# One attention-and-gating block on one core: the row maximum over two key blocks formed as relu of a score difference, kept in its PSUM bank, with the second scores accumulated onto it

## The chip, the cores and the metric

The kernel runs on one core of one Trainium2 chip. The metric is device microseconds (us) of one launch. The kernel before takes 1705.86 us (median of three runs, 1705.18 to 1706.04). Engine names here are those of the profile: PE is TensorE (PEld its weight loads), ACT is ScalarE, DVE is VectorE, POOL is GpSimd, SP issues most DMAs.

## The reference, cut to what matters

The block has 2048 rows of width 512, 32 heads of 16, and a gated MLP behind the attention.

```python
h  = x + softmax((ln(x) @ wq) @ (ln(x) @ wk).T * 16**-0.5) @ (ln(x) @ wv) @ wo   # 32 heads
z  = gelu(ln(h) @ w_in);  z1, z2 = z[:, :688], ln(z[:, 688:])
out = h + (z1 * (w_sp @ z2 + b_sp)) @ w_out
```

A softmax needs the maximum of each row of 2048 scores before its exponentials. This change concerns how that maximum is found.

## The kernel before, in words

**Stages.** The kernel first normalizes x and projects queries, keys and values (until about 158 us). Then it runs the attention proper (about 158 to 1300 us), then h and z row block by row block (about 1300 to 1455 us), then the spatial product and the output.

**Attention.** A unit is a group of four heads (`hg`), 512 queries (`qb`) and 128 keys (`kb`). The loop at L1086 takes two units at a time, 256 such rounds, in the order that the list `PAIR` (L40) writes out by hand:

```python
PAIR = "s0 M0 join s2 M4 M1 s1 H s3 invert M2 s5 M3 H out M5 s4 M7 turn s6 s7 M6 P".split()
```

- `s0` to `s7` (L846) are the eight score matmuls of the two units. Each fills one of three PSUM banks `s`, and ACT exponentiates it into `pt` in SBUF (L855).
- `H` (twice) weighs the values of the second unit of the round before with half of the columns each, `P` those of this round's first unit (L871): four float32 matmuls, eight rows in the trace, on bank `pv`.
- `M0` to `M7` are the steps of `max_pair` (L205). They find the row maxima of 128 queries of two heads, one of each kind named below, and run eleven rounds ahead of the scores that need them.
- `out` copies `pv` away on DVE (L881, once in eight rounds), `invert`, `join` and `turn` do small work on DVE, each once in eight rounds.

**The row maxima.** The four heads of a unit are of two kinds, `t` = 0 and 1, which lie on different halves of PE's rows (0 to 49 and 64 to 113). So a matmul of one kind can run beside one of the other. A step makes the scores of 128 queries for 512 keys in a bank `m0` to `m3` (L223), and DVE takes the maximum of each row (`reduce_max`, L228). For `t` = 1 that is done for all four blocks of keys (M0, M4, M5, M7), for `t` = 0 for the last two (M1, M2). The first two blocks of `t` = 0 go by max(a, b) = (a + b + |a - b|) / 2. Keys are added and subtracted beforehand (`uvs`, made in `sums`, L480, and loaded by `load_uv`, L170). M3 (`minus`, L230) makes a - b, and ACT writes |a - b| to an SBUF tile `ab` (L233). M6 (`plus`, L235) makes a + b in another bank, and DVE adds `ab`, halves and takes the maximum in one custom instruction (L237), followed by one that reads its accumulator.

**Banks and queues.** Each step takes the next of the four `m` banks in turn (L1145). In a round, M0, M4, M1, M2, M3, M5, M7, M6 take banks 0, 1, 2, 3, 0, 1, 2, 3. Instructions stand on every engine in the order in which the program gives them; a matmul that waits holds up the matmuls behind it.

**Before and after the loop.** The first eleven rounds' worth of maxima are found during the projections (`ahead`, L544), in calls of five or four steps. The last eleven rounds have no `M` steps. In the z stage the pool `mid_ps` (L1220) has six banks, shared by the four accumulators of z in a row block and the one of h (L1310).

In what follows a prime marks the round that comes next: s0' is its first score matmul.

Of the kernel before, what the change touches and what calls it, by code (L numbers as in the profile page):

```python
# [19 lines left out]
P = 128  # L20
# [39 lines left out]
def block_kernel(ctx: ExitStack, tc: tile.TileContext, x, wqkv, wo, w_in, w_sp4, b_sp, w_out, out):  # L60
# [20 lines left out]

    q_scr = dram.tile([2, H * DH, S], F16, name="q_scr")
    k_scr = dram.tile([2, H * DH, S], F16, name="k_scr")
    uv_scr = dram.tile([2, DB, P // 2, 2, 512], F16, name="uv_scr")
    v_scr = dram.tile([S, D], F32, name="v_scr")
    o_scr = dram.tile([DB, 8, 32, S], F32, name="o_scr")
    r_scr = dram.tile([H, S], F32, name="r_scr")
# [54 lines left out]
    VP = NB * 4 * VW  # L142
    vst = [vpool.tile([P, VP + DH], F32, name=f"vst{i}") for i in range(2)]
    kst = [kpool.tile([RG + KM, 2, S], F16, name="kst0")]
    uvs = [kpool.tile([KS, 2, 1024], F16, name="uvs0")]
    qst, mx, turned = {}, {}, {}

    def fixed(t):
# [21 lines left out]
    def load_uv(hg, pieces=range(3)):  # L170
        r = slice(32 * (hg % 2), 32 * (hg % 2) + 32)
        for j in pieces:
            nc.sync.dma_start(
                uvs[hg % 2][j:KS:3, :, :],
                uv_scr[(0, 0, 1)[j], hg // 2, r].rearrange("(p r) i s -> r p (i s)", r=DH))

    def load_v(hg):
        raw = vpool.tile([P, NB, 4 * DH], F32, name="raw")
# [26 lines left out]
    def max_pair(m):  # L205

        g, i = divmod(m, 8)
        hg, qb = divmod(g, NQ)
        q, k, w = qst[g], kst[hg % 2], uvs[hg % 2]
        if i == 0:
            mx[g] = sm.tile([P, 16, 4], F32, name="mx")
            nc.gpsimd.memset(mx[g][:, :8, 3:], LOW)
        c, p = slice(i % 4 * P, i % 4 * P + P), i // 4
        at = lambda t, e: mx[g][:, t * 8 + i, e:e + 1]

        def scores(t, keys, b):  # L220
            r = slice(RG * t, RG * t + KS)
            acc = bank(b)
            nc.tensor.matmul(acc, q[r, p, c], keys[r, p], start=True, stop=True)  # L223
            return acc

        def one(t, e, b):
            acc = scores(t, k[:, :, 512 * e:512 * e + 512], b)
            nc.vector.reduce_max(at(t, e if t else e - 1), acc, axis=AX.X)  # L228

        def minus(b):  # L230
            acc = scores(0, w[:, :, 512:], b)
            ab[0] = sm.tile([P, 512], F32, name="ab")
            nc.scalar.activation(ab[0], acc, AF.Abs)  # L233

        def plus(b):  # L235
            acc = scores(0, w[:, :, :512], b)
            nc.vector.tensor_tensor_reduce(ab[0], acc, ab[0], 0.5, LOW, ALU.add, ALU.max, at(0, 0))  # L237

        def finish():
            if i == 7:  # L240
                nm = sm.tile([P, 2, 8], F32, name="nm")
                nc.vector.tensor_reduce(nm.rearrange("p t i -> p (t i)"), mx.pop(g), axis=AX.X,  # L242
                                        op=ALU.max, negate=True)
                parts = sm.tile([P, 2, 2, 8], F16, name="mparts")
                nc.gpsimd.tensor_scalar(nm, nm, 1.0 / ONE, 1.0, op0=ALU.mult, op1=ALU.mult)  # L245
                nc.gpsimd.tensor_copy(parts[:, :, 0], nm)
                nc.gpsimd.tensor_sub(parts[:, :, 1], nm, parts[:, :, 0])
                turned[0] = (g, parts)

        ab = {}  # L250
        four = [lambda b, e=e: one(1, e, b) for e in range(4)]
        two = [lambda b, e=e: one(0, e, b) for e in (2, 3)]
        return [four[0], two[0], two[1], minus, four[1], four[2], plus, four[3], finish]

    def max_rows():

# [12 lines left out]
    with ExitStack() as pre:  # L269
# [188 lines left out]
        def proj_qk(b, n, which, between=lambda d: None):  # L458

            c = slice(n * 512, (n + 1) * 512)  # L460
            acc = next_acc()
            for d in range(DB):
                mm3(acc, wqk[b][0][:, which, d, :], wqk[b][1][:, which, d, :],
                    xT[0][:, d, c], xT[1][:, d, c], d == 0, d == DB - 1)
                between(d)

            def take(by_act=True):
                part = p2.tile([P, 2, 512], F16, name="part", bufs=PB)
                if by_act:
                    nc.scalar.activation(part[:, 0, :], acc, AF.Copy, scale=QK_DOWN)  # L470
                else:
                    nc.vector.tensor_scalar(part[:, 0, :], acc, QK_DOWN, None, op0=ALU.mult)
                nc.vector.scalar_tensor_tensor(part[:, 1, :], acc, QK_DOWN, part[:, 0, :],
                                               op0=ALU.mult, op1=ALU.subtract)
                scr = (q_scr, k_scr)[which]
                nc.sync.dma_start(scr[:, b * P:(b + 1) * P, c].rearrange("i p s -> p i s"), part)
                if which == 1 and n < 2:
                    rest.append(sums)

            def sums():  # L480
                hh = P // 2
                if which == 1 and n < 2:
                    kf[n] = p2.tile([P, 512], F32, name=f"kf{n}", bufs=1)
                    nc.scalar.activation(kf[n][:hh], acc[:hh], AF.Copy, scale=QK_DOWN)
                    nc.scalar.activation(kf[n][hh:], acc[:hh], AF.Copy, scale=-QK_DOWN if n else QK_DOWN)
                if which == 1 and n == 1:
                    uv = p2.tile([P, 512], F32, name="uv", tag="row", bufs=10)
                    nc.gpsimd.tensor_add(uv, kf[0], kf[1])
                    part = p2.tile([P, 2, 512], F16, name="part", bufs=PB)
                    nc.gpsimd.tensor_copy(part[:, 0, :], uv)  # L490
                    nc.gpsimd.tensor_sub(part[:, 1, :], uv, part[:, 0, :])
                    for i in range(2):
                        nc.sync.dma_start(uv_scr[:, b, :, i, :].rearrange("i p s -> p i s"),
                                          part[hh * i:hh * i + hh])

            return take

# [46 lines left out]
        def ahead(k):  # L544
            for _ in range(k):
                m = done[0] // 8
                if not todo and m < LEAD:
                    steps = max_pair(m)
                    todo.extend(steps[i] for i in (0, 1, 4, 2, 5, 3, 6, 7))
                    ends.append(steps[8])  # L550
                if todo:
                    todo.pop(0)(done[0] % 5)
                    done[0] += 1
                    if not todo:
                        ends.pop()()
# [273 lines left out]
    with ExitStack() as at:  # L829
        kpool1 = at.enter_context(tc.tile_pool(name="kpool1", bufs=1))  # L830
        kst.append(kpool1.tile([RG + KM, 2, S], F16, name="kst1"))
        uvs.append(kpool1.tile([KS, 2, 1024], F16, name="uvs1"))
        fixed(kst[1])
        pp = at.enter_context(tc.tile_pool(name="pp", bufs=6))
        ps_v = at.enter_context(tc.tile_pool(name="ps_v", bufs=1, space=PSUM))
# [381 lines left out]
    with ExitStack() as mid:  # L1217
        m2 = mid.enter_context(tc.tile_pool(name="mid_2", bufs=2))
        zs, zst = {}, {}
        ps = mid.enter_context(tc.tile_pool(name="mid_ps", bufs=6, space=PSUM))  # L1220

        def new_z(sb):
            zs[sb] = [m2.tile([P, FH], F32, name=f"z{i}", bufs=1 + 3 * i) for i in range(2)]
# [75 lines left out]
        with tc.manual_schedule(engines={E.PE, E.Activation, E.DVE, E.Pool, E.SP}):  # L1299
            asked.pop(0)()  # L1300
            load_row(row[4])
            for k in range(NB):
                sb, new = row[k], row.get(k + 2)
                if k >= NB - 2:
                    scale_z(row[k - 1])
                    gate_z(row[k - 1])
                if k + 4 < NB:
                    asked.pop(0)()
                if k and new is not None:
                    for _ in make_h(new, ps.tile([P, 512], F32, name="acc")):  # L1310
                        pass
                if k + 3 < NB:
                    split_o(row[k + 3])
                if k + 5 < NB:
                    asked.append(load_o(row[k + 5]))
                new_z(sb)
                for c in range(2):
                    make_z(sb, 1, c)
                if new is not None:
                    mv, rs = scale_h(new)  # L1320
                    nb = minus_mean(e2, mv, rs)
                mean_z(sb)
                if 0 < k < NB - 2:
                    scale_z(row[k - 1])
                if new is not None:
                    hns[new] = e2.tile([P, D], F32, name="hn")
                    nc.scalar.activation(hns[new], xrs.pop(new), AF.Identity, bias=nb, scale=rs)
                    halve_h(new)
                spread_z(sb)
                if new is not None:  # L1330
                    turn_h(new)
                if subs:
                    subs.pop()(nc.vector)
                if k + 5 < NB:
                    load_row(row[k + 5])
                if k % 2:
                    ask()
                for c in range(2):
                    make_z(sb, 0, c)
                nc.scalar.dma_start(z_scr[sb * P:(sb + 1) * P, :], zs[sb][0])  # L1340
                hTs.pop(sb)
                if k == 1:
                    invert()
                if 0 < k < NB - 2:
                    gate_z(row[k - 1])
# [319 lines left out]
```

## Time and profile before

| | |
|---|---|
| median of three runs | 1705.86 us |
| the profiled execution | 1703.25 us |
| its span (first to last instruction) | 1701.5 us |
| mean granted PE clock | 1.00 |
| exponentials on ACT (L855), attention | 1968, mean 638 ns |
| row maxima on DVE (L228) | 1510, mean 682 ns |
| the custom instruction on DVE (L237) | 252 with `m` banks, mean 676 ns |
| absolute values on ACT (L233) | 252 with `m` banks, mean 626 ns |

A row of the timeline gives a start, a length, the engine, the line, the operation, output and inputs with shapes, and how many instructions were merged. A length is from start to end of an instruction: on all three engines the next one starts before the last has ended, so the distance of two starts is shorter than a length. Here the distance of two starts, or of two ends, in a full queue is called a slot.

### The profile page before, as it was taken

To read this page: it belongs to the slowest core of one execution; us is meant where nothing else is said; L and a number is where in the kernel's file an instruction comes from. 1 tells how busy PE (TensorE), PEld (TensorE's weight loads), DVE (VectorE), ACT (ScalarE), POOL (GpSimd) and SP (SyncE) were. 2 spreads that over 40 slices of the span, in tenths; PEclk is the share of its full clock that TensorE was granted. 3 is DMA by queue.
4 is the path that set the end of the run, shared out by engine and by line. 5 is a ranking of instruction groups with operands and counts; after the bars stand their busy time and mean duration, and the time that the engine had idled before them with its cause. 6 is when DMAs were issued, how large, how long until landed. Compare 5 with 4: busy or idle time off the path is not lost.

```text
span 1701.5 us, 36391 instructions
## 1 busy us (share of the span) xinstructions
PE 1687.1 (99%) x13410; PEld 634.3 (37%) x13410; DVE 1431.4 (84%) x3011; ACT 1338.1 (79%) x2648; POOL 821.8 (48%) x1070
## 2 busy tenths in 40 slices
PE   9999999999999999999999999999999999999999
PEld 4433222222222222222222222222224666666665
DVE  7588999999999999999999999999955776543444
ACT  4335999999999999999999999999996677211111
POOL 1522867776673266687767777400001778200100
PEclk9999999999999999999999999999999999999999
DMA  5744332343221244344443544300116775664551
GB/s 186 205 113 143 99 89 80 91 94 85 79 66 26 57 119 118 92 147 133 123 124 105 147 143 127 87 14 13 40 34 150 203 198 144 235 229 157 202 215 44
DMA packets 214138, 202.29 MB, mean 119 GB/s; under 512 B 92328, under 2 KB 164840, under 8 KB 213960
## 3 DMA queue, kind: packets, MB, share of 16 engines
q1 hardware_dynamic: 211656, 194.33, 39.9%
q10 hardware_dynamic: 2304, 5.64, 1.1%
q8 instruction: 105, 1.72, 0.4%
q14 instruction: 73, 0.60, 0.1%
HBM read 122.10 MB, written 65.93 MB: 111 GB/s over the span
## 4 chain that ended last, share of the span: by engine, by line
PE 85%; DVE 8%; POOL 2%; DMA 2%; ACT 1%; issue 1%; SPq 1%; POOLq 0%; ACTq 0%
PE pv L871 26%; PE s L846 18%; PE m L223 10%; DVE mx L228 6%; PE acc L107 5%; PE acc L109 5%; PE acc L108 5%; PE g L107 4%; PE g L108 4%; PE g L109 4%; PE acc L772 2%; DVE og L881 1%; DVE ab L237 1%; ACT pt L855 1%; DMA raw<-in_w_sp 0%
## 5 line engine op out<-in xcount | busy, mean ns | idle before, releaser
L855 ACT ACTIVATE pt<-s 128x512 f32<-128x512 f32 x1968 | 1007.1, 638 | 2.7 <-PE m L223 1.5
L228 DVE TENSOR_REDUCE mx<-m 128x1 f32<-128x512 f32 x1510 | 947.0, 682 | 11.8 <-PE m L223 3.0
L846 PE MATMUL s<-qst,kst 50*128 50x512 f16 x2048 | 604.2, 379 | 0.1
L871 PE MATMUL pv<-pt,vst 128*32 128x256 f32 (+1 forms) x6056 | 598.2, 466 | 4.1 <-DVE og L881 1.2
L223 PE MATMUL m<-kst,qst 48*128 48x512 f16 x1510 | 452.4, 381 | 0.1
L846 PEld LDWEIGHTS <-kst 50*128 50x128 f16 x2048 | 131.8, 94 | 352.0 <-issue 323.6
L871 PEld LDWEIGHTS pv<-pt,vst 128*32 128x32 f32 x6056 | 119.5, 108 | 290.0 <-issue 276.6
L223 PEld LDWEIGHTS <-qst 48*128 48x128 f16 x2048 | 159.4, 93 | 174.5 <-issue 124.0
L223 PE MATMUL m<-uvs,qst 48*128 48x512 f16 x504 | 190.7, 380 | 0.4 <-DVE mx L228 0.4
L245 POOL TENSOR_SCALAR nm<-nm 128x16 f32<-128x16 f32 x32 | 6.5, 204 | 361.2 <-DVE nm L242 361.2
L237 DVE CUSTOM_DVE_ANT_0 ab<-m,ab 128x512 f32<-128x512 f32 x252 | 170.3, 676 | 2.7 <-ACT ab L233 2.7
L233 ACT ACTIVATE ab<-m 128x512 f32<-128x512 f32 x252 | 157.8, 626 | 15.8 <-PE m L223 15.1
L1429 ACT ACTIVATE pr<-pr,up 128x304 f32<-128x304 f32 (+1 forms) x32 | 17.0, 574 | 108.7 <-DVE up L1383 108.7
L1032 POOL TENSOR_TENSOR op<-raw,op 128x512 f16<-128x512 f32 x80 | 92.8, 1160 | 6.1
L955 POOL TENSOR_TENSOR raw<-raw 128x512 f32<-128x512 f32 (+1 forms) x84 | 83.1, 989 | 6.7
L960 POOL TENSOR_TENSOR acc_sp<-acc_sp,raw 128x512 f32<-128x512 f32 x63 | 80.3, 1275 | 4.5
L107 PE MATMUL acc<-wi,hT 128*128 128x344 f16 x256 | 79.1, 309 | 3.0 <-DVE xr L776 3.0
L109 PE MATMUL acc<-wi,hT 128*128 128x344 f16 x256 | 79.1, 309 | 0.0
L108 PE MATMUL acc<-wi,hT 128*128 128x344 f16 x256 | 79.1, 309 | 0.0
L1571 POOL TENSOR_TENSOR pr<-pr,z 128x344 f32<-128x344 f32 x8 | 7.3, 910 | 148.4 <-DMA whole<-squares 108.3
L952 POOL TENSOR_SCALAR raw<-raw 128x512 f32<-128x512 f32 (+1 forms) x88 | 52.1, 592 | 19.8 <-DMA raw<-in_wqkv 12.5
L1570 DVE TENSOR_TENSOR pr<-g,v 128x344 f32<-128x344 f32 x8 | 4.1, 516 | 66.3 <-PE g L109 63.5
(253 smaller groups left out, 2280.5 us busy)
## 6 DMA issues: line engine op xcount, KB each, us to landing
raw<-in_w_sp SPq DMA_DIRECT2D x128, 256.0 KB
s_scr<-op SPq DMA_DIRECT2D x64, 256.0 KB
op<-s_scr SPq DMA_DIRECT2D x32, 512.0 KB
a_scr<-op SPq DMA_DIRECT2D x48, 256.0 KB
op<-a_scr SPq DMA_DIRECT2D x24, 512.0 KB
o_scr<-og SPq DMA_DIRECT2D x64, 128.0 KB
qst<-q_scr SPq DMA_DIRECT2D x192, 32.0 KB
kst<-k_scr SPq DMA_DIRECT2D x48, 128.0 KB
```

The costliest lines, as they stand in the source:

```text
L107: nc.tensor.matmul(ps, lh, rh, start=first, stop=False, **kw)
L108: nc.tensor.matmul(ps, lh, rl, start=False, stop=False, **kw)
L109: nc.tensor.matmul(ps, ll, rh, start=False, stop=last, **kw)
L223: nc.tensor.matmul(acc, q[r, p, c], keys[r, p], start=True, stop=True)
L228: nc.vector.reduce_max(at(t, e if t else e - 1), acc, axis=AX.X)
L233: nc.scalar.activation(ab[0], acc, AF.Abs)
L237: nc.vector.tensor_tensor_reduce(ab[0], acc, ab[0], 0.5, LOW, ALU.add, ALU.max, at(0, 0))
L846: nc.tensor.matmul(s, kst[hg % 2][r, p, kb * P:(kb + 1) * P], qst[hg * NQ + qb][r, p, :], start=True, stop=True)
L855: nc.scalar.activation(pts[p, kb][:, t, :], s, AF.Exp, scale=scales_[hg // 2])
L871: nc.tensor.matmul(pv[0][32 * j:32 * j + 32, a:b], vst[hg % 2][:, c:c + 32], pts[j % 2, kb][:, j // 2, a:b], start=kb == 0, stop=kb == NB - 1,
L955: pool.tensor_mul(got[0] if n else acc, got[0], got[0])
L1032: chores.append((lambda: pool.tensor_sub(t[0][:, 1], of(), t[0][:, 0]), TT))
```

## The change

The difference a - b stays in its bank: ACT writes relu(a - b) over it in place (step 3, now `over`). Step 6, now `onto`, multiplies the queries with the second block of the keys themselves and accumulates onto the same bank: relu(a - b) + b = max(a, b). DVE takes the maximum with the same `reduce_max` as elsewhere. The sum of keys is no longer made, stored or loaded, and the tile `ab` is gone. `onto` takes no bank of its own, though the count that hands out banks still advances. `PAIR` is not changed. In the calls during the projections, step 3 now comes fourth and step 2 fifth. In the z stage, h has a bank of its own and z's accumulators five.

```diff
-        def minus(b):
-            acc = scores(0, w[:, :, 512:], b)
-            ab[0] = sm.tile([P, 512], F32, name="ab")
-            nc.scalar.activation(ab[0], acc, AF.Abs)
-
-        def plus(b):
-            acc = scores(0, w[:, :, :512], b)
-            nc.vector.tensor_tensor_reduce(ab[0], acc, ab[0], 0.5, LOW, ALU.add, ALU.max, at(0, 0))
+        def over(b):
+            both[0] = scores(0, w, b)
+            nc.scalar.activation(both[0], both[0], AF.Relu)
+
+        def onto(b):
+            r = slice(0, KS)
+            nc.tensor.matmul(both[0], q[r, p, c], k[r, p, 512:1024], start=False, stop=True,
+                             skip_group_check=True)
+            nc.vector.reduce_max(at(0, 0), both[0], axis=AX.X)
...
-        return [four[0], two[0], two[1], minus, four[1], four[2], plus, four[3], finish]
+        return [four[0], two[0], two[1], over, four[1], four[2], onto, four[3], finish]
...
                 if which == 1 and n < 2:
-                    kf[n] = p2.tile([P, 512], F32, name=f"kf{n}", bufs=1)
-                    nc.scalar.activation(kf[n][:hh], acc[:hh], AF.Copy, scale=QK_DOWN)
-                    nc.scalar.activation(kf[n][hh:], acc[:hh], AF.Copy, scale=-QK_DOWN if n else QK_DOWN)
+                    kf[n] = p2.tile([hh, 512], F32, name=f"kf{n}", bufs=1)
+                    nc.scalar.activation(kf[n], acc[:hh], AF.Copy, scale=QK_DOWN)
...
-                    todo.extend(steps[i] for i in (0, 1, 4, 2, 5, 3, 6, 7))
+                    todo.extend(steps[i] for i in (0, 1, 4, 3, 2, 5, 6, 7))
...
-        ps = mid.enter_context(tc.tile_pool(name="mid_ps", bufs=6, space=PSUM))
+        ps = mid.enter_context(tc.tile_pool(name="mid_ps", bufs=5, space=PSUM))
+        ps_h = mid.enter_context(tc.tile_pool(name="mid_h", bufs=1, space=PSUM))
...
-                    for _ in make_h(new, ps.tile([P, 512], F32, name="acc")):
+                    for _ in make_h(new, ps_h.tile([P, 512], F32, name="h")):
```

PE, from the last score matmul of a round (s7) over M6 and P to the first two matmuls of the next round (s0' and M0'), in the kernel before; a number behind a name tells one buffer from another:

```order
L846 LDWEIGHTS kst1_1822
L846 MATMUL s_9679<-qst_7925,kst1_1822 128x512 [waits Activation_49]
L223 LDWEIGHTS qst_8499
L223 MATMUL m3_9682<-uvs1_1823,qst_8499 128x512 [waits DVE_49]
L871 MATMUL pv_9685<-pt_9620,vst1_157 32x512 [waits DVE_49]
L871 MATMUL pv_9685<-pt_9627,vst1_157 32x512
L871 MATMUL pv_9685<-pt_9620,vst1_157 32x512
L871 MATMUL pv_9685<-pt_9627,vst1_157 32x512
L846 LDWEIGHTS kst1_1822
L846 MATMUL s_9722<-qst_7925,kst1_1822 128x512 [waits Activation_49]
L223 LDWEIGHTS qst_8499
L223 MATMUL m0_9725<-kst1_1822,qst_8499 128x512
```

The same place in the changed kernel:

```order
L844 LDWEIGHTS kst1_1788
L844 MATMUL s_9436<-qst_7729,kst1_1788 128x512 [waits Activation_49]
L236 LDWEIGHTS qst_8287
L236 MATMUL m0_9412<-kst1_1788,qst_8287 128x512 [waits Activation_49]
L869 MATMUL pv_9441<-pt_9378,vst1_157 32x512 [waits DVE_49]
L869 MATMUL pv_9441<-pt_9385,vst1_157 32x512
L869 MATMUL pv_9441<-pt_9378,vst1_157 32x512
L869 MATMUL pv_9441<-pt_9385,vst1_157 32x512
L844 LDWEIGHTS kst1_1788
L844 MATMUL s_9478<-qst_7729,kst1_1788 128x512 [waits Activation_49]
L223 LDWEIGHTS qst_8287
L223 MATMUL m0_9481<-kst1_1788,qst_8287 128x512 [waits DVE_49]
```

The rows stand in the same order. M6 writes bank 0, which M3 filled, and waits for ACT in place of DVE; M0', which takes bank 0 in its turn, now waits for DVE.

DVE, from M2's maximum over those of M5, M7 and M6 to M0', in the kernel before, in a round with the copy of `pv`:

```order
L228 TENSOR_REDUCE mx_9375<-m3_9647 128x1 [waits PE_49]
L881 COPY og_9662<-pv_9066 128x512 [waits PE_49]
L228 TENSOR_REDUCE mx_9375<-m1_9666 128x1 [waits PE_49]
L228 TENSOR_REDUCE mx_9375<-m2_9672 128x1 [waits PE_49]
L237 ISA ab_9656,mx_9375<-m3_9682,ab_9656 128x512 [waits PE_49,Activation_49]
L237 ISA mx_9375 128x1
L228 TENSOR_REDUCE mx_9375<-m0_9725 128x1 [waits PE_49]
```

The same place in the changed kernel:

```order
L228 TENSOR_REDUCE mx_9139<-m3_9405 128x1 [waits PE_49]
L879 COPY og_9419<-pv_8838 128x512 [waits PE_49]
L228 TENSOR_REDUCE mx_9139<-m1_9423 128x1 [waits PE_49]
L228 TENSOR_REDUCE mx_9139<-m2_9429 128x1 [waits PE_49]
L238 TENSOR_REDUCE mx_9139<-m0_9412 128x1 [waits PE_49]
L228 TENSOR_REDUCE mx_9139<-m0_9481 128x1 [waits PE_49]
```

One plain reduction stands in place of the custom instruction and its reader. The last maximum of a round and the first of the next read the same bank.

More of the change, by code (lines that the diff above doesn't have):

```diff
@@ L83, in block_kernel @@
     k_scr = dram.tile([2, H * DH, S], F16, name="k_scr")
-    uv_scr = dram.tile([2, DB, P // 2, 2, 512], F16, name="uv_scr")
+    uv_scr = dram.tile([2, DB, P // 2, 512], F16, name="uv_scr")
     v_scr = dram.tile([S, D], F32, name="v_scr")
@@ L144, in block_kernel @@
     kst = [kpool.tile([RG + KM, 2, S], F16, name="kst0")]
-    uvs = [kpool.tile([KS, 2, 1024], F16, name="uvs0")]
+    uvs = [kpool.tile([KS, 2, 512], F16, name="uvs0")]
     qst, mx, turned = {}, {}, {}
@@ L174, in load_uv @@
                 uvs[hg % 2][j:KS:3, :, :],
-                uv_scr[(0, 0, 1)[j], hg // 2, r].rearrange("(p r) i s -> r p (i s)", r=DH))
+                uv_scr[(0, 0, 1)[j], hg // 2, r].rearrange("(p r) s -> r p s", r=DH))
     def load_v(hg):
@@ L248, in finish @@
                 turned[0] = (g, parts)
-        ab = {}
+        both = {}
         four = [lambda b, e=e: one(1, e, b) for e in range(4)]
         two = [lambda b, e=e: one(0, e, b) for e in (2, 3)]
-        return [four[0], two[0], two[1], minus, four[1], four[2], plus, four[3], finish]
+        return [four[0], two[0], two[1], over, four[1], four[2], onto, four[3], finish]
     def max_rows():
@@ L482, in sums @@
                 if which == 1 and n < 2:
-                    kf[n] = p2.tile([P, 512], F32, name=f"kf{n}", bufs=1)
-                    nc.scalar.activation(kf[n][:hh], acc[:hh], AF.Copy, scale=QK_DOWN)
-                    nc.scalar.activation(kf[n][hh:], acc[:hh], AF.Copy, scale=-QK_DOWN if n else QK_DOWN)
+                    kf[n] = p2.tile([hh, 512], F32, name=f"kf{n}", bufs=1)
+                    nc.scalar.activation(kf[n], acc[:hh], AF.Copy, scale=QK_DOWN)
                 if which == 1 and n == 1:
-                    uv = p2.tile([P, 512], F32, name="uv", tag="row", bufs=10)
-                    nc.gpsimd.tensor_add(uv, kf[0], kf[1])
-                    part = p2.tile([P, 2, 512], F16, name="part", bufs=PB)
+                    uv = p2.tile([P, 512], F32, name="uv", tag="row", bufs=10)[:hh]
+                    nc.gpsimd.tensor_sub(uv, kf[0], kf[1])
+                    part = p2.tile([P, 2, 512], F16, name="part", bufs=PB)[:hh]
                     nc.gpsimd.tensor_copy(part[:, 0, :], uv)
                     nc.gpsimd.tensor_sub(part[:, 1, :], uv, part[:, 0, :])
-                    for i in range(2):
-                        nc.sync.dma_start(uv_scr[:, b, :, i, :].rearrange("i p s -> p i s"),
-                                          part[hh * i:hh * i + hh])
+                    nc.sync.dma_start(uv_scr[:, b].rearrange("i p s -> p i s"), part)
             return take
@@ L831, in block_kernel @@
         kst.append(kpool1.tile([RG + KM, 2, S], F16, name="kst1"))
-        uvs.append(kpool1.tile([KS, 2, 1024], F16, name="uvs1"))
+        uvs.append(kpool1.tile([KS, 2, 512], F16, name="uvs1"))
         fixed(kst[1])
```

## The prediction

> **What bounds the kernel now.** I read the page first, then the windows, the groups and at last one round of the timeline. The page says that PE is busy in 99% of the span, and its chain of waits runs over PE:
>
> ```profile
> PE 1687.1 (99%) x13410; PEld 634.3 (37%) x13410; DVE 1431.4 (84%) x3011; ACT 1338.1 (79%) x2648; POOL 821.8 (48%) x1070
> PE 85%; DVE 8%; POOL 2%; DMA 2%; ACT 1%; issue 1%; SPq 1%; POOLq 0%; ACTq 0%
> ```
>
> That is an average over stages. The first row below is a window from the middle of the attention loop (busy time and instructions of PE, PEld, DVE, ACT, POOL): three engines have no gap. The others are from the views of L237 and L881 inside the loop (shortest, median and longest in ns, then the first and the last start).
>
> ```profile
> 600.00:800.00 200.00, 198.95 (x1800) 56.29 (x1792) 197.72 (x384) 199.18 (x405) 143.54 (x191) 1.00 0.42 119
> L237 DVE CUSTOM_DVE_ANT_0 ab<-m,ab x245: 644/680/683, 162.1 to 1246.1; 128x512 f32<-128x512 f32 x123
> L881 DVE COPY og<-pv x7: 678/679/680, 231.8 to 444.7; 128x512 f32<-128x512 f32 x7
> ```
>
> ACT has 200 / 405 = 0.494 us for each instruction. L237 counts the rounds that the change touches: 245, (1246.1 - 162.1) / 244 = 4.443 us apart. The copies of `pv` come once in eight rounds, (444.7 - 231.8) / 6 = 35.48 us apart. What sets this pace is seen in a single round. ACT first: the exponential of s5, then |a - b|, then four exponentials (s4, s6, s7, s0'), and the last two of these alone:
>
> ```profile
> 724.41 0.61 ACT L855 ACTIVATE pt<-s 128x512 f32<-128x512 f32 x1
> 724.88 0.62 ACT L233 ACTIVATE ab<-m 128x512 f32<-128x512 f32 x1
> 725.36 2.10 ACT L855 ACTIVATE pt<-s 128x512 f32<-128x512 f32 x4
> 726.32 0.66 ACT L855 ACTIVATE pt<-s 128x512 f32<-128x512 f32 x1
> 726.81 0.66 ACT L855 ACTIVATE pt<-s 128x512 f32<-128x512 f32 x1
> ```
>
> PE in the same round: M5, s7, M6, P, s0' and, later, s1':
>
> ```profile
> 724.60 0.39 PE L223 MATMUL m<-kst,qst 48*128 48x512 f16 x1
> 725.07 0.37 PE L846 MATMUL s<-qst,kst 50*128 50x512 f16 x1
> 725.07 0.39 PE L223 MATMUL m<-uvs,qst 48*128 48x512 f16 x1
> 725.39 1.06 PE L871 MATMUL pv<-pt,vst 128*32 128x512 f32 x8
> 726.39 0.39 PE L846 MATMUL s<-qst,kst 50*128 50x512 f16 x1
> 727.03 0.37 PE L846 MATMUL s<-qst,kst 50*128 50x512 f16 x1
> ```
>
> A queued ACT instruction takes a slot of 0.49 us: |a - b| ends at 725.50, the four behind it at 727.46, 1.96 / 4. Nine of them, eight exponentials and |a - b|, make 4.41 us. PE is tied to ACT in a ring: s7 starts at 725.07, just behind the end of s5's exponential (724.41 + 0.61 = 725.02), whose bank it takes. P follows at 725.39, s0' at 726.39 and the exponential of s0' at 726.81, just 0.17 before s7's ends (726.32 + 0.66 = 726.98). So ACT's queue is all but empty when s0' is done: whatever delays P by more than a trifle stops ACT.
>
> **The change, part by part.** *The wait at M6.* Today |a - b| ends at 725.50, and M6 has been running in another bank since 725.07, 0.43 earlier. In the new program M6 adds onto the very bank that ACT rewrites, and waits for it. A page of the Trainium skill speaks against this change (PSUM — Partial Sum Buffer, "PSUM bank collisions raise a hardware error"): no two engines may touch one bank at the same time, so M3, Relu, M6 and the maximum must follow one another. By that rule alone the 0.43 of overlap would be lost in each round, an estimate of 105 us in 245; the trace has no two engines in one `m` bank at once, so it neither bears the rule out nor denies it.
>
> Queued behind M6 on PE stand P, s0', M0' and all else. So the new ring, from one Relu's end to the next, goes as follows. Relu's end to M6 takes 0.05 (as from 725.02 to 725.07), M6 to P 725.39 - 725.07 = 0.32, P to s0' 726.39 - 725.39 = 1.00, and s0' to its exponential 726.81 - 726.39 = 0.42. That exponential takes 0.61, since it meets an idle engine, and then s2', s1', s3', s5' and Relu take five slots of 0.49, or 2.45. The sum is 4.85 us, against nine slots today. ACT has only the 1.47 us of s4, s6 and s7 left after Relu, while the way to the exponential of s0' takes 0.05 + 0.32 + 1.00 + 0.42 = 1.79.
>
> This ring holds if PE does not stop elsewhere in the round. The first half of another round (s0; M4 with M1; s1; the first H; s3; M5):
>
> ```profile
> 704.34 0.39 PE L846 MATMUL s<-qst,kst 50*128 50x512 f16 x1
> 704.57 0.59 PE L223 MATMUL m<-kst,qst 48*128 48x512 f16 x2
> 704.98 0.37 PE L846 MATMUL s<-qst,kst 50*128 50x512 f16 x1
> 705.28 0.64 PE L871 MATMUL pv<-pt,vst 128*32 128x256 f32 x8
> 705.85 0.39 PE L846 MATMUL s<-qst,kst 50*128 50x512 f16 x1
> 706.96 0.39 PE L223 MATMUL m<-kst,qst 48*128 48x512 f16 x1
> ```
>
> M1 starts at 704.57 + 0.59 - 0.38 = 704.78. s1, on the other rows of PE, could go beside it but starts 0.20 later, and the round above says why: s1' starts at 727.03, behind the end of s7's exponential (726.98), whose bank it takes. In the new ring that exponential ends 1.47 after Relu and s0' starts 1.37 after it, so s1' finds its bank free and the 0.20 goes. Then s3' starts 705.85 - 704.34 - 0.20 = 1.31 after s0', and its exponential could start at 1.31 + 0.42 = 1.73; ACT reaches it three slots after the exponential of s0', at 0.42 + 3 x 0.49 = 1.89. PE has 0.16 to spare there.
>
> *The wait at M0'.* Relu's bank is bank 0, which M0' takes next. It comes free when DVE has taken M6's maximum, the last of the round; today M0' needs only |a - b| done. DVE's rows for M5, M7 and M6:
>
> ```profile
> 725.02 0.69 DVE L228 TENSOR_REDUCE mx<-m 128x1 f32<-128x512 f32 x1
> 725.63 0.68 DVE L228 TENSOR_REDUCE mx<-m 128x1 f32<-128x512 f32 x1
> 726.23 0.68 DVE L237 CUSTOM_DVE_ANT_0 ab<-m,ab 128x512 f32<-128x512 f32 x1
> ```
>
> A maximum starts 725.02 - 724.60 = 0.42 after its matmul, and a slot on DVE is 0.60. From M0 to M5 it is 706.96 - 704.34 = 2.62 today, 2.42 without the 0.20. So from M0' to the next M0 it takes 2.42 + 0.42 + two slots + 0.68 for M6's maximum + 0.05 for the signal, 4.77 us. This second ring is 0.08 shorter than the first, and counts where DVE has other work:
>
> ```profile
> L881 DVE COPY og<-pv 128x512 f32<-128x512 f32 x24 | 16.3, 679 | 0.0
> L818 DVE RECIPROCAL rcp<-sums 128x16 f32<-128x16 f32 x24 | 5.8, 242 | 0.8 <-DMA sums<-o_scr 0.7
> L242 DVE TENSOR_REDUCE nm<-mx 128x16 f32<-128x64 f32 x24 | 5.0, 208 | 0.0
> L259 DVE STREAM_TRANSPOSE mturned<-mparts 128x32 f16<-128x32 f16 x24 | 4.8, 201 | 0.0
> ```
>
> The copy takes a slot, so M0' comes 0.60 - 0.08 = 0.52 late once in eight rounds; 0.16 of that PE can spare, 0.36 is lost. The reciprocal (0.24 - 0.08 = 0.16) is spared. The other two fall into one round: 0.41 - 0.08 - 0.16 = 0.17 at the most, nothing at the least; I take 0.06, as they overlap with their neighbours. Eight rounds take 8 x 4.85 + 0.36 + 0.06 = 39.22 against 8 x 4.443 = 35.54 today: 3.68 more, and 3.68 x 245 / 8 = 112.7 us.
>
> *The price of Relu* is not in the trace: no ACT row writes PSUM. I take that of |a - b| (0.62 long, slot 0.49), the nearest row: same input, shape and engine. The ends are the shortest and the longest plain row of 512 columns, 0.59 and 0.81:
>
> ```profile
> L485 ACT ACTIVATE kf<-acc 64x512 f32<-64x512 f32 x8 | 4.7, 588 | 0.1
> L413 ACT ACTIVATE xg<-xg,nb,rs_r 128x512 f32<-128x512 f32 x13 | 10.3, 805 | 13.9 <-DVE nb L402 7.1 <-issue 6.8
> 83.00:158.00 75.00, 74.87 (x369) 27.97 (x367) 63.23 (x119) 25.71 (x47) 18.29 (x25) 1.00 0.41 116
> 1300.00:1400.00 100.00, 100.00 (x628) 61.20 (x626) 71.97 (x245) 66.72 (x138) 63.66 (x71) 1.00 0.79 200
> ```
>
> That is 0.03 x 245 = 7 us less or 0.19 x 245 = 47 us more.
>
> *At nothing* I cost the rest. DVE's plain maximum replaces the custom instruction and its reader (0.68 against 0.68 and some), but DVE waits at the round's end now. The eight copies of L485 go (4.7 us), with half of the bytes of `uvs`: in their stage (third row above) ACT is busy 25.71 of 75 us and PE 74.87, so PE's projections hide them; without that cover the gain is at most the 4.7. There Relu and M6 fall into different calls, a projection apart, but for one call of five steps: 0.7 us once, against these savings. In the z stage (last row) PE is busy throughout; h's bank is read and free long before the next row block, so its own bank changes nothing, at worst one 0.68 on DVE in each of 14 row blocks, 10 us.
>
> The profiled execution took 1703.25 us (span 1701.5), and 1703.25 + 112.7 = 1816.0. The median shown is 2.6 above the profiled execution, so the forecast is 1705.86 + 112.7 = 1818.6 us.
>
> **The rivals.** *Faster: the wait is swallowed.* If M6's wait cost nothing, ACT's nine slots would remain, and Relu's could be shorter. The Trainium skill (ScalarE: Activation LUTs, "Step-by-step: what each stage is for") says that ScalarE writes PSUM faster than SBUF; no row here shows it. With the 0.59 end, 0.03 x 245 is 7 us less, about 1698. That decides once the 1.79 us from Relu's end to the exponential of s0' falls to 1.47 - 0.17 = 1.30, what ACT has queued less the overlap of two exponentials. P alone is 1.00 of it, and no row shows P shorter.
>
> *No change.* A round still has 8 + 8 matmuls beside P and H, nine ACT and seven DVE instructions of like length. If the new waits fall into slack, the time stays 1706. The ring above shows 0.17 of slack at s0', not 0.44.
>
> *Slower still: M0' takes the lead.* If s1' keeps its 0.20, the second ring is 4.97 and pays DVE's other work in full, 0.60 + 0.24 + 0.41 = 1.25 in lengths and about 1.0 with their overlap: 40.8 in eight rounds, 5.2 more, 160 us, 1866. Against it: s7's exponential ends too early to hold s1'.
>
> *Slower still: reading and writing one bank halves Relu's pace.* One more slot, 5.34 in a round: 7.2 more in eight, 220 us, 1926. Nothing in the trace speaks for it or against it.
>
> **How the numbers follow.** The forecast, with Relu between its ends, gets 0.80; M0' in the lead 0.07, the halved pace 0.05, the swallowed wait 0.05, no change 0.03. A measurement of this kernel can tell about 0.2% (3.4 us). Hence faster 0.05, same 0.03, slower 0.92. The range starts at 1818.6 - 7 less the whole 12.9 for DVE's other work (0.42 x 245 / 8), 1798, and takes in M0' in the lead and the long Relu, both at 1866.
>
> **What the new profile would show.** Right: rounds of L233's successor 4.85 us apart, copies of `pv` 39.2 apart; M6 starting 0.05 after Relu's end and P 0.32 behind it; ACT and DVE idle once in each round, ACT before s0''s exponential by some 0.4, DVE before M0's maximum; M0' held beside s0' after the copies. Wrong: M6 starting with s7, or rounds still near 4.44. If Relu is longer or shorter than 0.62, the first ring moves by just that, and only a shorter one meets the second ring at 4.77.

## The result and the profile after

The changed kernel takes 1809.19 us (median of five runs, 1808.93 to 1809.61), the kernel before beside it 1705.25 us. The ratio is 1.0613 (95% interval 1.0601 to 1.0624), 103.9 us more. The forecast was 112.7 more.

The page of the changed kernel: its span, and each engine's busy time, share and instructions, then the shares of the chain of waits, and the groups of the exponentials, of Relu, of M6's matmul and of the first matmuls of z's accumulators.

```profile
span 1807.8 us, 35869 instructions
PE 1763.9 (98%) x13410; PEld 644.9 (36%) x13410; DVE 1435.1 (79%) x2755; ACT 1363.6 (75%) x2640; POOL 821.4 (45%) x1070
PE 55%; ACT 33%; DVE 8%; issue 2%; POOL 1%; DMA 1%; SPq 0%; POOLq 0%; ACTq 0%
L853 ACT ACTIVATE pt<-s 128x512 f32<-128x512 f32 x1968 | 1029.9, 618 | 79.5 <-PE s L844 62.5
L232 ACT ACTIVATE m<-m 128x512 f32<-128x512 f32 x251 | 159.5, 635 | 20.1 <-PE m L223 20.1
L236 PE MATMUL m<-kst,qst 48*128 48x512 f16 x251 | 93.5, 373 | 29.5 <-ACT m L232 0.5
L107 PE MATMUL acc<-wi,hT 128*128 128x344 f16 x256 | 79.1, 309 | 0.0
```

PE still reads 98% busy, and 77 us more of it than before with the same 13410 matmuls. The matmuls have not grown longer: one of the scores takes 380 ns in the mean (379 before), one of M6 373. PE counts as busy as long as any matmul runs. M6 used to run beside s7 on the other half of PE's rows; now it runs by itself, 0.30 us up to P in the round shown below, and 0.30 x 245 = 74 us. PE's own idle time ahead of M6 is only 29.5 us. What tells is ACT, which had next to no gap before (2.7 us ahead of exponentials). Now it stands idle for 79.5 us there, and the chain goes over ACT for a third of the span.

Where the time went is read from the view of the exponentials' line, one row for each kernel (shortest, median and longest length in ns, then the first and the last start). First the kernel before:

```profile
L855 ACT ACTIVATE pt<-s x1968: 592/648/686, 157.8 to 1250.3; 128x512 f32<-128x512 f32 x197
```

Then the changed kernel, with the same view of M6's maximum (inside the loop) and of the copies of `pv` (first seven), and the loop's middle as in the window shown of before:

```profile
L853 ACT ACTIVATE pt<-s x1968: 592/607/663, 160.1 to 1359.5; 128x512 f32<-128x512 f32 x197
L238 DVE TENSOR_REDUCE mx<-m x245: 645/681/692, 164.5 to 1355.0; 128x1 f32<-128x512 f32 x123
L879 DVE COPY og<-pv x7: 681/681/681, 202.0 to 436.2; 128x512 f32<-128x512 f32 x7
600.00:800.00 200.00, 194.12 (x1644) 53.36 (x1640) 181.90 (x316) 186.83 (x370) 117.49 (x162) 1.00 0.34 94
```

The spans of the two profiled executions differ by 1807.8 - 1701.5 = 106.3 us. Ahead of the first exponential it is 160.1 - 157.8 = 2.3 more. From the first to the last it is 1199.4 against 1092.5, 106.9 more. Behind the last it is 448.3 against 451.2, 2.9 less. So the whole loss lies in the loop. A round takes (1355.0 - 164.5) / 244 = 4.879 us, eight rounds (436.2 - 202.0) / 6 = 39.03 (4.443 and 35.48 before). ACT gets through 370 instructions in the 200 us of the window where it did 405.

One round in the changed kernel, ACT first: s3 and s5, Relu, then s4, s6 and s7, a gap of 0.29, and s0' with the next four.

```profile
723.33 1.11 ACT L853 ACTIVATE pt<-s 128x512 f32<-128x512 f32 x2
724.28 0.65 ACT L232 ACTIVATE m<-m 128x512 f32<-128x512 f32 x1
724.80 1.61 ACT L853 ACTIVATE pt<-s 128x512 f32<-128x512 f32 x3
726.70 2.56 ACT L853 ACTIVATE pt<-s 128x512 f32<-128x512 f32 x5 [0.29 <-PE s L844]
```

PE in the same round: M6, P, s0', M0', s1', and the M6 of the next round.

```profile
724.98 0.37 PE L236 MATMUL m<-kst,qst 48*128 48x512 f16 x1
725.28 1.06 PE L869 MATMUL pv<-pt,vst 128*32 128x512 f32 x8
726.28 0.39 PE L844 MATMUL s<-qst,kst 50*128 50x512 f16 x1
726.38 0.37 PE L223 MATMUL m<-kst,qst 48*128 48x512 f16 x1
...
726.81 0.38 PE L844 MATMUL s<-qst,kst 50*128 50x512 f16 x1
...
729.80 0.37 PE L236 MATMUL m<-kst,qst 48*128 48x512 f16 x1
```

Relu ends at 724.28 + 0.65 = 724.93. M6 starts 0.05 later, P 0.30 after that, s0' 1.00 after P, its exponential 0.42 after s0'. The next M6 comes 729.80 - 724.98 = 4.82 after this one. This is the first ring of the prediction, step for step.

DVE there: M6's maximum, then M0's.

```profile
725.64 0.68 DVE L238 TENSOR_REDUCE mx<-m 128x1 f32<-128x512 f32 x1
726.79 1.89 DVE L228 TENSOR_REDUCE mx<-m 128x1 f32<-128x512 f32 x3 [0.46 <-PE m L223]
```

M6's maximum ends at 726.32, M0' starts at 726.38, 0.10 behind s0': the second ring is close behind the first. Where it leads, the waits of PE in the loop show it (total, times, longest):

```profile
PE m L223 <- DVE mx L238: 6.0, 29, 0.2
```

Some 30 rounds, one in eight, have the copy of `pv`.

### The profile page after: what moved, and what is told of

It is laid out like the page before. It is cut to its first block, busy times and chain, and to the rows that moved or that the text cites. A ratio compares the mean times of both kernels' runs of the same rounds, so it can differ in the third digit from the quotient of the medians.

```text
span 1807.8 us, 35869 instructions
## 1 busy us (share of the span) xinstructions
PE 1763.9 (98%) x13410; PEld 644.9 (36%) x13410; DVE 1435.1 (79%) x2755; ACT 1363.6 (75%) x2640; POOL 821.4 (45%) x1070
## 4 chain that ended last, share of the span: by engine, by line
PE 55%; ACT 33%; DVE 8%; issue 2%; POOL 1%; DMA 1%; SPq 0%; POOLq 0%; ACTq 0%
ACT pt L853 27%; PE pv L869 14%; ACT m L232 6%; DVE mx L228 6%; PE s L844 5%; PE acc L107 5%; PE acc L109 5%; PE acc L108 5%; PE m L236 4%; PE g L107 4%; PE g L108 4%; PE g L109 4%; PE h L770 2%; PE m L223 2%; DVE mx L238 1%
## 5 line engine op out<-in xcount | busy, mean ns | idle before, releaser
L853 ACT ACTIVATE pt<-s 128x512 f32<-128x512 f32 x1968 | 1029.9, 618 | 79.5 <-PE s L844 62.5
L228 DVE TENSOR_REDUCE mx<-m 128x1 f32<-128x512 f32 x1511 | 939.8, 683 | 120.5 <-PE m L223 91.0
L223 PE MATMUL m<-kst,qst 48*128 48x512 f16 x1511 | 424.9, 379 | 6.2 <-DVE mx L238 6.2
L844 PEld LDWEIGHTS <-kst 50*128 50x128 f16 x2048 | 147.3, 93 | 379.9 <-issue 336.3
L223 PEld LDWEIGHTS <-qst 48*128 48x128 f16 x1792 | 133.7, 93 | 128.5 <-issue 109.4
L232 ACT ACTIVATE m<-m 128x512 f32<-128x512 f32 x251 | 159.5, 635 | 20.1 <-PE m L223 20.1
L238 DVE TENSOR_REDUCE mx<-m 128x1 f32<-128x512 f32 x251 | 170.0, 677 | 0.0
L236 PE MATMUL m<-kst,qst 48*128 48x512 f16 x251 | 93.5, 373 | 29.5 <-ACT m L232 0.5
L223 PE MATMUL m<-uvs,qst 48*128 48x512 f16 x251 | 94.4, 376 | 0.0
L935 POOL TENSOR_SCALAR raw<-raw,figs 128x512 f32<-128x512 f32 (+1 forms) x84 | 55.5, 665 | 10.5 <-DMA raw<-in_wo 8.7
```

The costliest lines, as they stand in the source:

```text
L232: nc.scalar.activation(both[0], both[0], AF.Relu)
L236: nc.tensor.matmul(both[0], q[r, p, c], k[r, p, 512:1024], start=False, stop=True, skip_group_check=True)
L238: nc.vector.reduce_max(at(0, 0), both[0], axis=AX.X)
L844: nc.tensor.matmul(s, kst[hg % 2][r, p, kb * P:(kb + 1) * P], qst[hg * NQ + qb][r, p, :], start=True, stop=True)
L853: nc.scalar.activation(pts[p, kb][:, t, :], s, AF.Exp, scale=scales_[hg // 2])
```

## The experiments

Each ratio is against the kernel before, run beside it. The pace of a round is worked out from the view of M6's maximum in each kernel, as above: last start less first start, by 244.

**Relu's bank apart (1794.71 us, ratio 1.0531, 1.0515 to 1.0547).** The changed kernel with a table of banks. M6 still waits for Relu; M0' no longer needs a bank that DVE reads last.

```diff
+BANK = (0, 2, 0, 3, 1, 1, 3, 2)
...
-                    steps[i](count[0] % 4)
+                    steps[i](BANK[i])
```

> The changed kernel with the order of steps as it is, but with banks given out by a table, so that Relu's bank (3) is taken next by M3 of the next round and M0' takes M2's (0). M6 still waits for Relu. Theory (two rings, M6's wait the longer): rounds fall to a flat 4.82 us, the late M0' after the copy of pv goes, eight rounds take 38.6 in place of 39.03, so 13 us less than the changed kernel, about 1796. Rival 1 (the bank that M0' waits for is the whole cost): back to about 1706. Rival 2 (Relu in place is itself the cost): no change, 1809.

```profile
L239 DVE TENSOR_REDUCE mx<-m x245: 643/679/692, 163.5 to 1339.7; 128x1 f32<-128x512 f32 x123
```

The pace is 4.820, just the distance of two M6 in the round above, and no wait of PE for a maximum is left in the loop. The first ring alone makes nearly the whole loss; the second adds 1809.19 - 1794.71 = 14.5 us, as the paces also say: (4.879 - 4.820) x 245 = 14.5.

**Relu earlier (1803.69 us, 1.0582, 1.0568 to 1.0597).** If M6's wait is the cause, an earlier Relu should end it. M2 and M3 change places:

```diff
-PAIR = "s0 M0 join s2 M4 M1 s1 H s3 invert M2 s5 M3 H out M5 s4 M7 turn s6 s7 M6 P".split()
+PAIR = "s0 M0 join s2 M4 M1 s1 H s3 invert M3 s5 M2 H out M5 s4 M7 turn s6 s7 M6 P".split()
```

> The changed kernel with M2 and M3 exchanged in the hand-written order. Relu then stands ahead of the exponential of s5, so M6, which runs beside s7, waits for nothing that s7 does not wait for; and since the banks are dealt in turn, M0' takes M2's bank and no longer Relu's. Theory: both waits go, rounds are back at 4.41 to 4.44, 1700 to 1707. Rival 1 (only the bank counts): the same. Rival 2 (Relu in place holds ACT longer): still over 1790, with ACT without a gap and a slot of Relu over 0.9.

This failed. ACT (Relu now ahead of s5, then s5, s4, s6, s7, a gap, s0') and PE (s7, M6, P):

```profile
725.75 0.63 ACT L232 ACTIVATE m<-m 128x512 f32<-128x512 f32 x1
726.26 2.08 ACT L853 ACTIVATE pt<-s 128x512 f32<-128x512 f32 x4
728.68 0.60 ACT L853 ACTIVATE pt<-s 128x512 f32<-128x512 f32 x1 [0.33 <-PE m L223]
```

```profile
726.93 0.37 PE L844 MATMUL s<-qst,kst 50*128 50x512 f16 x1 [0.48 <-ACT pt L853]
726.94 0.39 PE L236 MATMUL m<-kst,qst 48*128 48x512 f16 x1
727.26 1.06 PE L869 MATMUL pv<-pt,vst 128*32 128x512 f32 x8
```

Relu ends at 726.38, M6 starts at 726.94 beside s7: it waits for nothing. But s7 now waits for the exponential of s5, whose bank it takes and which stands one slot later on ACT, behind Relu. P comes as late as before. So the cause has to be put more widely. PE holds P until some ACT instruction is done, M6 by Relu or s7 by the exponential of s5. What counts is how many ACT instructions lie from the exponential of s0' to the one that P stands behind: five in the kernel before, six here and in the changed kernel. With five, the prediction's own steps give 0.05 + 0.32 + 1.00 + 0.42 + 0.61 + 4 x 0.49 = 4.36, just under the nine slots of 4.41. With six it is 4.85.

**The same exchange in the kernel before (1802.75 us, 1.0575, 1.0559 to 1.0591).** There is no Relu, and nothing is accumulated onto a bank that ACT wrote; only the line of the diff above is changed.

> The kernel before, with nothing changed but M2 and M3 exchanged in the hand-written order: no Relu, no shared bank, no wait of M6 for ACT. The exchange puts the absolute value ahead of the exponential of s5 on ACT. Theory (mended after the exchange in the changed kernel: P stands behind s7, s7 behind the exponential of s5, and what counts is how many ACT instructions lie between the exponential of s0' and the one that P stands behind; six here, five before): rounds of 4.855 us, 245 x (4.855 - 4.443) = 101 us more, 1803 to 1808. Rival (Relu in the bank, or M6's wait for it, is the cost in itself): no change, 1703 to 1706.

The view of the custom instruction, then the page's group of score matmuls with their idle time:

```profile
L237 DVE CUSTOM_DVE_ANT_0 ab<-m,ab x245: 644/681/692, 162.7 to 1343.6; 128x512 f32<-128x512 f32 x123
L846 PE MATMUL s<-qst,kst 50*128 50x512 f16 x2048 | 603.8, 379 | 113.1 <-ACT pt L855 113.1
```

|a - b| and the exponentials of s5, s4, s6 and s7 on ACT, then s7, M6, P and s0' on PE, in one round:

```profile
727.23 0.63 ACT L233 ACTIVATE ab<-m 128x512 f32<-128x512 f32 x1
727.71 2.11 ACT L855 ACTIVATE pt<-s 128x512 f32<-128x512 f32 x4
728.40 0.37 PE L846 MATMUL s<-qst,kst 50*128 50x512 f16 x1 [0.46 <-ACT pt L855]
728.41 0.39 PE L223 MATMUL m<-uvs,qst 48*128 48x512 f16 x1
728.72 1.06 PE L871 MATMUL pv<-pt,vst 128*32 128x512 f32 x8
729.72 0.39 PE L846 MATMUL s<-qst,kst 50*128 50x512 f16 x1
```

A pace of 4.840 and 97.9 us, from one exchange in the order. M6 takes the bank of |a - b| here, since banks are dealt in turn, but |a - b| ends at 727.86 and M6 starts at 728.41 with s7: what holds PE is the exponential of s5. The pace and the time lie just under what was expected. The mended reason holds.

**Still earlier, in the kernel before (1802.95 us, 1.0562, 1.0545 to 1.0580).** M1 and M3 change places (`M4 M3 s1 H s3 invert M1 s5 M2`), which puts |a - b| two places earlier on ACT than the exchange above; the count stays six, and M6 has the bank of M1.

> The kernel before with M1 and M3 exchanged, so that M3 and the absolute value come two exponentials earlier than in the exchange of M2 and M3. Theory (the first ring counts the ACT instructions between the exponential of s0' and that of s5, wherever the sixth stands): the same 4.84 a round as there, 1801 to 1804. Rival (the distance of M3 from s7 counts, an earlier M3 is harmless): 1703 to 1710.

```profile
L237 DVE CUSTOM_DVE_ANT_0 ab<-m,ab x245: 649/683/684, 162.8 to 1344.2; 128x512 f32<-128x512 f32 x123
```

4.842: it is the count that matters, not how early M3 is.

**The second ring, in the kernel before (1813.48 us, 1.0627, 1.0609 to 1.0644).** M6 and M2 share M0's bank, M3 has its own. M0' waits for the last work of DVE; M6 waits for nothing new.

```diff
+BANK = (0, 2, 0, 3, 1, 1, 0, 2)
...
-                    steps[i](count[0] % 4)
+                    steps[i](BANK[i])
```

> The kernel before, order and arithmetic as they are, only banks given out by a table: M3 has bank 3 to itself, and M2 and M6 have bank 0, so M0' waits for DVE's last work of the round before, as in the changed kernel. M6 and P wait for nothing new. Theory (the second ring exists by itself): from M0' to the next M0 4.78 us in plain rounds, DVE's other work nearly in full (5.3 with the copy of pv), 39.0 to 39.4 in eight rounds, 245 x (4.88 to 4.93 - 4.443) = 107 to 119 us more, 1811 to 1824. Rival (M6's wait is the whole cost, M0' finds its bank free in time): 1703 to 1706.

```profile
L238 DVE CUSTOM_DVE_ANT_0 ab<-m,ab x245: 649/682/685, 162.7 to 1354.7; 128x512 f32<-128x512 f32 x123
```

The waits of PE in the loop:

```profile
PE m L224 <- DVE mx L238: 31.1, 148, 0.4
```

Alone it gives 4.885 a round, 107.5 us. So each ring by itself costs about what the change costs. They run side by side, and the longer one sets the pace; the losses don't add.

**Both, with Relu early (1815.00 us, 1.0649, 1.0633 to 1.0665).** The changed kernel with M2 and M3 exchanged as above and `BANK = (0, 2, 3, 0, 1, 1, 0, 2)`: Relu in bank 0, M0' waits for M6's maximum.

> As the exchange of M2 and M3, but with banks given out by a table so that M3, and so Relu, has bank 0, which M0' takes. M6's wait is gone, M0' still waits for M6's maximum. Theory: the second ring alone, 4.77 to 4.97 a round and DVE's other work (about 1.0 in eight rounds) in full: 39.2 to 40.8 in eight rounds, 1818 to 1866; that is as slow as the changed kernel though half of the cause is away, since the rings run side by side and do not add. Rival 1 (M6's wait is the whole cost): 1700 to 1707. Rival 2 (Relu itself): 1809.

The time is below the band expected, and the run rests on the reading that an early Relu ends the first ring, which the exchange of M2 and M3 disproves. So it does not show the second ring alone. Its pace is 4.902, from (1360.1 - 164.1) / 244, a little above either ring. What makes the last 0.02 was not followed up.

**Relu to SBUF (1699.72 us, 0.9974, 0.9963 to 0.9984).** The rest of the change stays: sums of keys gone, relu, h's own bank. Relu goes to a tile `ab` in SBUF, M6 makes b in a bank of its own, and DVE adds and takes the maximum.

```diff
-            both[0] = scores(0, w, b)
-            nc.scalar.activation(both[0], both[0], AF.Relu)
+            acc = scores(0, w, b)
+            both[0] = sm.tile([P, 512], F32, name="ab")
+            nc.scalar.activation(both[0], acc, AF.Relu)
...
+            acc = scores(0, k[:, :, 512:1024], b)
+            nc.vector.tensor_tensor_reduce(both[0], acc, both[0], 1.0, LOW, ALU.add, ALU.max, at(0, 0))
```

> The changed kernel with Relu written to an SBUF tile, M6 in a bank of its own and the custom instruction of before with factor 1: max(a, b) = relu(a - b) + b by DVE. All other edits stay (half of the key sums gone, order of the calls in the projections, h's own bank). Theory: the time of before, within 3 us: 1702 to 1708. Rival (the edits in the projections or in the z stage carry part of the loss): over 1709.

```profile
600.00:800.00 200.00, 199.36 (x1808) 56.70 (x1805) 198.37 (x384) 199.81 (x407) 145.02 (x193) 1.00 0.42 118
```

ACT is full again, 407 instructions in 200 us. All of the loss hangs on Relu in place with M6 onto it. This version beats both kernels, and lies 2.3 us under the band expected; the next experiment says why.

**h's bank alone, in the kernel before (1700.91 us, 0.9977, 0.9968 to 0.9987).** Only the lines on `mid_ps`, `mid_h` and h's tile of the change's diff.

> The kernel before, with only the z stage's edit: h in a bank of its own, five for z's accumulators. All theories: within 0.1% of the kernel before, 1703 to 1706; if it is slower or faster, the difference belongs to neither ring.

No theory expected a difference, and there is one: 4.0 us less. The page of the kernel before has one wait in the z stage, ahead of the first matmul of an accumulator:

```profile
L107 PE MATMUL acc<-wi,hT 128*128 128x344 f16 x256 | 79.1, 309 | 3.0 <-DVE xr L776 3.0
```

PE waits 3.0 us, once, for DVE to read h from a bank of the shared pool. In this version, as in the changed kernel above, the same group has no idle time. That is 3.0 of the 4.0 us; the other 1.0 is too small to place. The version with Relu in SBUF is 4.2 below its own reference, so nearly all of its gain is this edit too.

**M6 behind P (1760.14 us, 1.0323, 1.0307 to 1.0339).** The changed kernel with `s7 P M6` for `s7 M6 P` and the first table of banks above: P stands behind s7 alone, so the count is five again.

> The changed kernel with M6 behind P in place of ahead of it, and the table of banks that frees M0'. P stands behind s7 alone, and M6 comes when Relu has long ended, but takes a matmul's turn of PE by itself between P and s0' (0.21). Theory: from s5's exponential 0.05 to s7, 0.32 to P, 1.00, 0.21 for M6, 0.42 to the exponential of s0', 2.56 from its start to the end of s5' exponential: 4.56 a round, 245 x (4.56 - 4.443) = 29 us over the kernel before, 1733. Rival (Relu in place costs ACT): 1790 or more.

PE behind P, in one round, and the waits of PE in the loop:

```profile
744.27 1.06 PE L870 MATMUL pv<-pt,vst 128*32 128x512 f32 x8
745.27 0.39 PE L237 MATMUL m<-kst,qst 48*128 48x512 f16 x1
745.27 0.39 PE L224 MATMUL m<-kst,qst 48*128 48x512 f16 x1
745.50 0.38 PE L845 MATMUL s<-qst,kst 50*128 50x512 f16 x1
```

```profile
PE pv L870 <- DVE og L880: 15.1, 30, 0.6
```

s0' shares its half of PE's rows with M6 and starts 1.23 after P in place of 1.00. The ring of five becomes 4.36 + 0.23 = 4.59; seven rounds between two copies of `pv`, first M6 at 731.9 and last at 759.5, give 27.6 / 6 = 4.60:

```profile
L239 DVE TENSOR_REDUCE mx<-m x7: 690/691/692, 731.9 to 759.5; 128x1 f32<-128x512 f32 x7
```

The ring was as expected, the total 27 us above it: once in eight rounds P, which no longer stands behind Relu, waits for the copy of `pv`, 15.1 us in 30 waits, and the plain round is 0.04 above the 4.56 assumed, 10 us. That is 25 of the 27.

**M6 a round later (1732.15 us, 1.0157, 1.0143 to 1.0171).** The changed kernel with M3 behind s7 and M6 of the round before beside s3 (a list carries the steps over), the same table of banks, `join` after M6.

```diff
+PAIR = "s0 M0 s2 M4 M1 s1 H s3 invert M6 join s5 M2 H out M5 s4 M7 turn s6 s7 M3 P".split()
...
-    sums_ = {}
+    sums_, held = {}, []
...
+                elif tok == "M6":
+                    if held:
+                        held[0][6](3)
+                        joins.append(held.pop()[8])
...
```

> The changed kernel with M6 put off into the next round, beside s3, where it waits for nothing, and M3 beside s7, so that Relu comes behind all exponentials of its round; Relu's bank is its own (3). M6 of a round is followed there by the small work at the end of a query block. Only in the last round M6 stands where it stood. Theory: both rings are gone, DVE has 0.03 us less in a round, ACT sets the pace with nine slots: 4.41 to 4.44 a round, 1696 to 1702. Rival (Relu in place, PSUM to PSUM, holds ACT longer than a slot of 0.49): each 0.1 us of it shows as 24 us more.

ACT from one Relu to the next, and P in a round with the copy:

```profile
740.24 0.62 ACT L233 ACTIVATE m<-m 128x512 f32<-128x512 f32 x1
740.75 4.07 ACT L854 ACTIVATE pt<-s 128x512 f32<-128x512 f32 x8
744.70 0.62 ACT L233 ACTIVATE m<-m 128x512 f32<-128x512 f32 x1
```

```profile
744.51 1.06 PE L870 MATMUL pv<-pt,vst 128*32 128x512 f32 x8 [0.75 <-DVE og L880]
```

The wait at M6 is gone and a round is 744.70 - 740.24 = 4.46 on ACT, near nine slots. Three quarters of the loss come back with Relu in place and M6 onto it. What is left is above all P waiting for the copy, since M6's maximum now stands between those of M1 and M2, ahead of the copy on DVE: the copy starts 453.06 - 449.60 = 3.46 behind s0 in one such round, in the kernel before 444.75 - 441.89 = 2.86. It is 20.4 us by the waits of PE in the loop.

```profile
PE pv L870 <- DVE og L880: 20.4, 30, 0.8
```

That was not foreseen, and the expectation of no loss was missed.

## Why the prediction was right, and where it was off

*The wait at M6* was right in mechanism and nearly in size. Its ring was to be 4.85; alone it measures 4.820, and its steps read 0.05, 0.30, 1.00 and 0.42. M6 to P is 0.02 shorter than between s7 and P before, the rest is within the rounding of the rows. The gap on ACT was said to be some 0.4; it is 0.29, near what the prediction's own 1.79 - 1.47 gives.

What the prediction did not see is that the wait was not the whole reason. It found that ACT's queue is all but empty when s0' is done, but did not work out the ring that is already there: 4.36 against 4.41. One more ACT instruction on it costs 97 to 98 us in the two kernels with an exchanged order, with no wait of M6 at all.

*The wait at M0'* was right: 29 waits at M0', and 14.5 us on top of the first ring where DVE's other work was priced at 12.9. Eight rounds take 39.03 against 39.22 forecast.

The rival *M0' in the lead* rested on s1' keeping its 0.20. It starts 726.81 - 726.28 = 0.53 behind s0', where it was 0.64; what stays is about M0's own 0.10. So it found its bank free, and the time stayed far below 1866.

*The price of Relu* was taken as that of |a - b|. The two kernels with M2 and M3 exchanged have the same order, and their paces differ by 4.856 - 4.840 = 0.016 (the first from (1349.0 - 164.1) / 244):

```profile
L238 DVE TENSOR_REDUCE mx<-m x245: 645/679/691, 164.1 to 1349.0; 128x1 f32<-128x512 f32 x123
```

So Relu in place is about 0.02 dearer, 4 us in 245 rounds, inside the bounds and on the dear side. The rows of those two kernels show where. Relu and |a - b| are both 0.63 long, but the exponential behind starts 726.26 - 725.75 = 0.51 after Relu and 727.71 - 727.23 = 0.48 after |a - b|. With Relu to SBUF it is 0.47 to 0.48 (724.46 to 724.93 and 728.87 to 729.35 in that kernel), so the dearer part goes with the writing of PSUM.

The rival *faster* fell with that and with P, which is 1.00 from s0' as before. The Trainium skill's sentence that ScalarE writes PSUM faster than SBUF (ScalarE: Activation LUTs, "Step-by-step: what each stage is for") is not borne out by these traces. The halved pace fell too: no slot more.

*The rule on banks.* By the rule that engines take turns in a bank (the Trainium skill, PSUM — Partial Sum Buffer, "PSUM bank collisions raise a hardware error") and the 0.43 of overlap in the trace, the prediction estimated 105 us, close to the 103.9 measured. The agreement is chance. M3, Relu, M6 and the maximum follow one another in one bank in the kernel with M6 a round later as well, and there it costs 27 us. With no such chain in one bank, one exchange costs 97 to 98.

*At nothing.* The z stage gained 2.9 where the prediction gave h's own bank nothing. It read PE's busy share of the window, and missed the 3.0 in the group's idle column. In the projections, the one call of five steps shows two waits of PE:

```profile
PE tp L223 <- DVE mx L238: 0.9, 1, 0.9
PE m L236 <- ACT m L232: 0.5, 1, 0.5
```

That is 1.4 where 0.7 was priced; the first exponential comes 2.3 later. The other 0.9 is there before any maximum is taken: the first matmul of the values' projection, behind a wait for `xT`, starts at 48.49 against 47.56 in the kernel before. The eight copies spared bring nothing to be seen, as said.

*The sum.* 112.7, less 0.19 x 245 / 8 = 5.8 for the shorter eight rounds, less 2.9 in z, and 2.3 more in the projections are 106.3, the difference of the spans. The profiled execution of before lies 2.0 under the median of its runs, that of the changed kernel 0.4 above: 103.9.

## What to carry to other kernels

Before a wait is put on an engine, write down the ring that is already there: from the instruction that it gates, through the other engine's queue, back to what it waits for. If that ring is within one slot of the pace, as here (4.36 against 4.41), one instruction more between the two ends costs, in every round, what then sticks out above the pace (0.40 of its slot of 0.49 here), whether it brings a wait or not, and moving the waiting instruction out of the ring brings most of it back. The two rings on this loop don't add, so undoing one of them showed little of what it is worth alone.

## What the runs showed of the hardware

Matmuls on the two halves of PE's rows can pass each other. In the kernel with M6 behind P the program has M6, s0', M0' in this order; M0' starts with M6 at 745.27, s0', on M6's half, 0.23 later. A matmul that waits for another engine, by contrast, holds up P behind it: P stays 0.30 behind M6 in the changed kernel, and where P alone was put ahead of M6, with the banks of the first experiment, a plain round fell from 4.82 to 4.60.

An ACT instruction that writes 128x512 float32 to PSUM is not faster here than one that writes SBUF: both are 0.63 long in the same order, and the instruction behind the one to PSUM starts 0.03 later.
